# An attention and two feed-forward layers on one core: TensorE tile work in other groups, one PSUM pair shared in another way

## The chip, the cores and the metric

One core of one Trainium2 chip runs the whole program. The metric is the device time of one execution in microseconds; the kernel before took 1379.79 us, the median of three runs (1379.1 to 1381.74).

## The reference

```python
a   = softmax(phi, axis=2)                       # over 576 tokens, per memory slot
k_m = einsum('bhsm,bhsd->bhmd', a, k)            # 32 memory rows per head
v_m = einsum('bhsm,bhsd->bhmd', a, v)
attn = softmax(q @ k_m.T / 8, axis=-1)           # 576 x 32 per head
x = (attn @ v_m).transpose(0, 2, 1, 3).reshape(4608, 512)
h = x @ w_in;  x = (h * sigmoid(h)) @ w_out      # 512 -> 2048 -> 512
h = x @ w_in2; g = where(h > 0, h, exp(min(h, 0)) - 1)
out = g @ w_out2
```

There are 8 batches of 8 heads, 576 tokens, head width 64 and 32 memory slots. The weights come in as float64.

## The kernel before

**Stages.** A stretch written out by hand (FIRST) does batch 0's attention and first layer and brings in the first layer's weights. A planned stretch, about 97 to 703 us of the trace, then does the rest of batch 0, the attention and the first feed-forward layer of batches 1 to 7, and converts and splits the second layer's weights. A last stretch does the second feed-forward layer, nine blocks of 512 tokens.

**What sets the order.** `Plan` holds tasks with an engine, a cost, a rank and what they depend on, and `run` simulates the engines and issues every instruction in the order that comes out of it; on the chip each engine runs its instructions in that order. In the planned stretch the large products of TensorE get due times in order (`by_due`), and every other task must be ready 35 us (`AHEAD`) before the product that needs it. A `ring` stands for a buffer: a new user waits for the release by the user some places before it, and for the task that made the last one.

**Large products.** TensorE multiplies in float16 as three terms (`mm3`). `plan_in1` makes h = x·w_in for one batch as 16 products of 12 matmuls of 288 columns (tile `ph<-aT,u`); `plan_out1` multiplies by w_out with seven products in place of eight (`ph<-T,w1s`). Both use two PSUM slots `m0` and `m1` of two banks each.

**The attention of one batch, all between those products.**
- `mem_T` turns exp(phi) by transposes (`eT`; the last 64 tokens are `etail`), `mem_es` copies them out. `mem_kv` multiplies by k and v (`kvp`): ten chunks a batch, each four matmuls on four column tiles of 32, in one task with its own load (`kv`, three buffers). The last chunk of each half of the heads has 64 tokens, so 64 rows.
- `mem_pad`, `mem_kvT`, `mem_vT` scale and turn the result (`kvTp`, `kT`, `vT`).
- `scores` (`sc`) multiplies q by kT on two column tiles of 64: for each 64-token piece c, all four pairs of heads p, so four matmuls in a row on one tile. `att_*` make the softmax, `att_T` turns it back (`aTp`), `att_split` writes `aT`. Tokens come in three parts j of 256, 256 and 64; the part of 64 uses half of the partitions.
- `u_mm` (`up`) folds v_m into w_in: for each quarter f of the 2048 columns and each half g of the heads, eight matmuls of 512 columns on four column tiles of 32, one task each. `u_split` makes float16 hi and lo on ScalarE and VectorE (tile `u`). One `u` serves one batch; the next batch's overwrites it after the last product that reads it.

**PSUM.** Eight banks: four for `m0`, `m1`; two for tag `a` (`sc`, `aTp`), one for `u` (`up`), one for `c` (`eT`, `kvp`, `kvTp`). In FIRST and in the last stretch `a_tile` deals the same four in turn:

```python
if turn[1]:
    tag = "aauc"[k]
return ps_a.tile(shape, F32, tag=tag, name=name, bufs=2 if tag == "a" else 1)
```

Of the kernel before, what the change touches and what calls it, by code (L numbers as in the profile page):

```python
# [18 lines left out]
P = 128  # L19
B, H, S, D, M = 8, 8, 576, 64, 32  # L20
DM, DFF = 512, 2048
NG = 2
# [22 lines left out]
W2FROM, W2TO, AHEAD = 0.2, 0.95, 35  # L45
# [46 lines left out]
def attn_moe_moe(ctx: ExitStack, tc: tile.TileContext, qT, phiT, kvm, kvt, w1i, w1o, w2i, w2o, out):  # L92
# [37 lines left out]
    def a_tile(shape, name, tag="a"):  # L130

        k = turn[0] % 4
        turn[0] += turn[1]
        if turn[1]:
            tag = "aauc"[k]
        return ps_a.tile(shape, F32, tag=tag, name=name, bufs=2 if tag == "a" else 1)
# [65 lines left out]
    class Plan:  # L202
# [3 lines left out]
        def __init__(self, ahead=None, busy={}):  # L206
            self.tasks = []
            self.rings = {}
            self.gates = {}
            self.ahead = ahead  # L210
            self.busy = busy
            self.due = None
            self.main = []
            self.dues = {}
# [8 lines left out]
        def product(self, cost, rank, fn, deps=()):  # L223
            self.main.append(len(self.tasks))
            return self.add("PE", cost, rank, fn, deps)
# [39 lines left out]
        def run(self):  # L265
# [16 lines left out]
            order = []  # L282
            while len(order) < n:
# [18 lines left out]
                _, cost, _, fn, _, hold = self.tasks[i]  # L302
                end = start + cost
# [328 lines left out]

    def load_phi(b):
# [4 lines left out]
    def load_kv(b, g, c):  # L638

        t = two.tile([P, 4 * 2 * D], F32, tag="kv", name=f"kv{b}", bufs=NKV)  # L640
        if c < NC - 1:
            nc.sync.dma_start(out=t, in_=kvm[b, g, :, c])
        else:
            nc.sync.dma_start(out=t[:TAIL], in_=kvt[b, g])
        st[b]["kv", g, c] = t

    def load_kv_whole(b, tags):
        for g in range(NG):
# [4 lines left out]
            load_kv(b, g, NC - 1)  # L653
# [16 lines left out]
    def mem_T(b, g):  # L670

        z = st[b]
        if g < NG:
            ps = z["eT", g] = a_tile([P, NC - 1, P], "eT", "c")
            for c in range(NC - 1):
                nc.tensor.transpose(ps[:, c], z["phi"][:, g, c * P:(c + 1) * P], ident)  # L676
        else:
            ps = z["eT", g] = a_tile([P, NG, P], "etail", "c")
            for h in range(NG):
                nc.tensor.transpose(ps[:TAIL, h], z["phi"][:, h, (NC - 1) * P:], ident)  # L680

    def mem_es(b, g):
        z = st[b]
        if "es" not in z:
            z["es"] = big.tile([P, NG, NC, P], F32, tag="es", name=f"es{b}")
        ps = z.pop(("eT", g))
        if g < NG:
            copy("K0" if b else "T0", z["es"][:, g, :NC - 1], ps)
        else:
            copy("K0" if b else "T0", z["es"][:TAIL, :, NC - 1], ps[:TAIL])  # L690

    def mem_kv(b, g, c):
# [3 lines left out]
        r = P if c < NC - 1 else TAIL  # L696
        t = z.pop(("kv", g, c))
        for h in range(4):
            nc.tensor.matmul(  # L699
                z["kvp"][32 * h:32 * h + 32, g],  # L700
                z["es"][:r, g, c, 32 * h:32 * h + 32],
                t[:r, h * P:(h + 1) * P],
                start=(c == 0),
                stop=(c == NC - 1),
                tile_position=(0, 32 * h),
            )
# [76 lines left out]
    def tokens(j):  # L783

        return (P, 2) if j < 2 else (TAIL, 1)

    def scores(b, j):
        z = st[b]
        r, n = tokens(j)
        ps = z["sc", j] = a_tile([P, 2, H, M], "sc")  # L790
        for c in range(2 * n if j < 2 else 1):
            t0 = 256 * j + 64 * c
            o = 64 * (c % 2)
            for p in range(NP):
                nc.tensor.matmul(  # L795
                    ps[o:o + 64, c // 2, 2 * p:2 * p + 2],
# [7 lines left out]
    def att_max(b, j):  # L804
        z = st[b]
        r, n = tokens(j)
        sc = z["sc", j][:r, :n].rearrange("p n h m -> p (n h) m")
        z["smx", j] = small("smx", 16)
        nc.vector.tensor_reduce(out=z["smx", j][:r, :n * H], in_=sc, axis=AX.X, op=ALU.max)

    def att_sub(b, j):
        z = st[b]
        r, n = tokens(j)
        k = n * H
        sc = z.pop(("sc", j))[:r, :n].rearrange("p n h m -> p (n h) m")
        a = z["att", j] = two.tile(
            [P, 16, M], F32, tag="att" if b else "stage", name="att", bufs=2 if b else 4)
        tt(a[:r, :k], sc, z.pop(("smx", j))[:r, :k].unsqueeze(2).to_broadcast([r, k, M]), ALU.subtract)

    def att_exp(b, j):  # L820
        r, n = tokens(j)
        a = st[b]["att", j][:r, :n * H]
        nc.scalar.activation(out=a, in_=a, func=AF.Exp, scale=float(1.0 / np.sqrt(D)))

    def att_sum(b, j):
        r, n = tokens(j)
        k = n * H
        aa = st[b]["att", j][:r, :k]
        s1, s2 = small("ss1", 16), small("ss2", 16)
        st[b]["ss3", j] = small("ss3", 16)  # L830
        nc.vector.tensor_reduce(out=s1[:r, :k], in_=aa, axis=AX.X, op=ALU.add)
        nc.vector.tensor_scalar_add(s2[:r, :k], s1[:r, :k], 1e-9)
        nc.vector.reciprocal(st[b]["ss3", j][:r, :k], s2[:r, :k])

    def att_mul(b, j):
        r, n = tokens(j)
        k = n * H
        aa = st[b]["att", j][:r, :k]
        tt(aa, aa, st[b].pop(("ss3", j))[:r, :k].unsqueeze(2).to_broadcast([r, k, M]), ALU.mult)

    def att_T(b, j):
        z = st[b]
        r, n = tokens(j)
        a = z.pop(("att", j)).rearrange("p (n g h) m -> p n g (h m)", n=2, g=NG)
        ps = z["aTp", j] = a_tile([P, NG, 256], "aTp")
        for g in range(NG):
            for c in range(n):
                nc.tensor.transpose(ps[:, g, P * c:P * c + r], a[:r, c, g], ident[:r, :r])  # L848

    def att_split(b, j, lo):  # L850
        z = st[b]
        r, n = tokens(j)
# [3 lines left out]
        t = slice(256 * j, 256 * j + n * r)  # L856
        ps = z["aTp", j][:, :, :n * r]
# [23 lines left out]
    def u_mm(b, f, g):  # L881
# [3 lines left out]
        ps = z["up", f, g] = a_tile([P, FW], "up", "u")  # L885
# [26 lines left out]

    def plan_mem(pl, n, r, ex, ready):
# [10 lines left out]
        for g in range(NG + 1):  # L924
            t = on("PE", 0.5 if g < NG else 0.3, lambda g=g: mem_T(n, g), ex + pl.ring(*C))
            free = pl.take("c", t)
            phi_free.append(t)
            es.append(on("ACT", act(512 if g < NG else 256, False), lambda g=g: mem_es(n, g),
# [6 lines left out]
        for g in range(NG):  # L935
            for c in range(NC):
                load, free = [], []
                if n > 1:
                    load = [pl.load(256 if c < NC - 1 else 128, r - 300, lambda g=g, c=c: load_kv(n, g, c), pl.ring("kv", NKV), KVLATE if c < NC - 1 else 3.0)]
                    free = pl.take("kv", load[0])  # L940
                elif c == NC - 1:
                    free = pl.rings["kv"][1 + g][1]
                t = on("PE", 0.3, lambda g=g, c=c: mem_kv(n, g, c), load + es + (last or pl.ring(*C)))
                if not last:
                    kv_free = pl.take("c", t)
                last = [t]
                free.append(t)
            kv += last
# [25 lines left out]
    def plan_u(pl, n, r, mem, ready):  # L974
# [4 lines left out]
        for f in (0, 2, 1, 3) if n == 1 else range(NF):  # L979
            for g in range(NG):  # L980
                t = pl.add("PE", 0.55, r, lambda f=f, g=g: u_mm(n, f, g), [mem["vl"], ready["w1i", f]] + pl.ring("u", 1) + (
                    pl.ring(f"u{g}", 1) if f == 0 else [u[0, g]]))
                mem["vT_free"].append(t)
                free = pl.take("u", t)
# [7 lines left out]
    def plan_attn(pl, n, r, mem, after):  # L992


        A = "a", 2
# [10 lines left out]
        for j in range(3):  # L1006
            rows, w = tokens(j)
            k = 256 * w
            sc = on("PE", 1.8 if j < 2 else 0.5, lambda j=j: scores(n, j), [mem["kT"]] + qs + pl.ring(*A))
# [12 lines left out]
            t = on("PE", 0.6 if j < 2 else 0.3, lambda j=j: att_T(n, j), [t] + pl.ring(*A))  # L1022
# [39 lines left out]
    mslot = [0]  # L1062

    def ps_half(k):
        ps = ps_m.tile([P, 2, 512], F32, tag=f"m{k}", name="ph")
# [51 lines left out]
    def plan_in1(pl, b, r, A, u, u_free, first, h_free):  # L1117
# [4 lines left out]
        silus = []  # L1122
        at = mslot[0]

        def mm(m):
            w[m], ps = ps_half((at + m) % 2)
# [9 lines left out]
        for m in range(KF):  # L1136
            t = pl.product(1.475, r + m, lambda m=m: mm(m), A["aT"] + [u[m // 4, g] for g in range(NG)] + pl.ring(f"m{(at + m) % 2}", 1))
            for free in u_free + [A["aT_free"]]:
                free.append(t)
            free = pl.take(f"m{(at + m) % 2}", t)  # L1140
            silus.append(pl.add("ACT", act(S) - 0.02, r + m - 2000, lambda m=m: silu(m), [t, A["scales"]] + (silus[-1:] or first) + h_free(m)))
            free.append(silus[-1])
# [68 lines left out]
    def plan_out1(pl, b, r, silus, made, stored, scales, y_tile, y_ring, squares_rank=0):  # L1211
# [10 lines left out]
        SLOT = mslot[0], 1 - mslot[0]  # L1222
        mslot[0] = SLOT[1]
# [419 lines left out]
    def first_steps():  # L1643
# [29 lines left out]
        f["K0"] = lambda: ([mem_kv(0, g, c) for g in range(NG) for c in range(NC)], [mem_pad(0, g) for g in range(NG)])  # L1673
# [9 lines left out]
    def plan_first():  # L1683
# [79 lines left out]
        for k in range(NT):  # L1763
            pl.take("T", None).extend([ready["kv", 1][k]] if k < 2 else reads[3] + [done[KD - 1, 3]])
# [40 lines left out]
    with tc.manual_schedule():  # L1805
# [7 lines left out]
        turn[1] = 1  # L1813
        early.close()
# [78 lines left out]
```

## Time and profile before

| | us | share |
|---|---|---|
| median of three runs | 1379.79 | |
| the profiled execution | 1379.99 | |
| its span in the profile | 1378.2 | 1 |
| PE (TensorE) busy | 1351.3 | 98% |
| DVE (VectorE) busy | 1107.6 | 80% |
| ACT (ScalarE) busy | 952.3 | 69% |

The time of an execution holds 1.8 us around the span. A matmul's row shows its whole passage through the array, so rows of consecutive matmuls overlap; how long a block holds TensorE is read from its start to the start of the next block. A float32 matmul shows as two instructions.

### The profile page before, as it was taken

How to read it: one execution, taken by the hardware profiler on the slowest of the kernel's cores; microseconds unless marked ns; L12 is line 12 of the kernel's file. 1: busy time of each engine (PE TensorE's matmuls, PEld its weight loads, DVE VectorE, ACT ScalarE, POOL GpSimd, SP SyncE). 2: the span in 40 equal slices, each digit the busy share in tenths (PEclk: the TensorE clock that was granted, in tenths of full speed). 3: DMA queues.
4: the chain of work that ended last, by engine and by line, in shares of the span. 5: the costliest groups of instructions: out<-in, count | busy, mean ns of one | idle time of the engine just before them, and what ended most of it. 6: DMA issues, size and time to landing. Idle time of an engine off the chain costs nothing.

```text
span 1378.2 us, 28737 instructions
## 1 busy us (share of the span) xinstructions
PE 1351.3 (98%) x12105; PEld 1095.5 (79%) x12105; DVE 1107.6 (80%) x1730; ACT 952.3 (69%) x1366; POOL 84.6 (6%) x147
## 2 busy tenths in 40 slices
PE   7998999999999999999999999999999999999998
PEld 4676677776767767676787888888888888888887
DVE  6687788696988989697869797888879797879784
ACT  4757674967868686785658675758676676767672
POOL 0033100001010000011000000000000000000000
PEclk8999999999999999999999999999999999999999
DMA  9475857368576647645394242333333241514230
GB/s 371 175 253 169 291 213 267 124 236 280 188 246 236 237 161 265 255 151 209 122 372 150 78 142 76 124 100 100 109 108 116 69 154 43 171 53 134 87 99 31
DMA packets 65729, 233.07 MB, mean 169 GB/s; under 512 B 9024, under 2 KB 15168, under 8 KB 60992
## 3 DMA queue, kind: packets, MB, share of 16 engines
q1 hardware_dynamic: 53120, 187.19, 39.9%
q0 software_dynamic: 12480, 44.05, 8.4%
q8 instruction: 94, 1.54, 0.5%
q14 instruction: 35, 0.29, 0.1%
HBM read 186.12 MB, written 40.89 MB: 165 GB/s over the span
## 4 chain that ended last, share of the span: by engine, by line
PE 74%; DMA 3%; issue 3%; ACT 1%; DVE 1%; POOL 0%; ACTq 0%; SPq 0%; POOLq 0%
PE ph L1048 24%; PE o L1048 23%; PE h2A L1048 13%; PE h2D L1048 10%; DMA wi<-w2is 1%; PE sc L795 1%; DMA kv<-in_kvm 1%; PE up L889 1%; DMA w2is<-hl_q 1%; PE kvp L699 1%; PE aTp L848 0%; ACT h L1133 0%; DVE hl_q L189 0%; POOL w2is L468 0%; PE eT L676 0%
## 5 line engine op out<-in xcount | busy, mean ns | idle before, releaser
L1048 PE MATMUL o<-t,wq 128*128 128x256 f16 x3024 | 358.2, 273 | 0.1
L1048 PEld LDWEIGHTS <-wi 128*128 128x128 f16 x3024 | 295.6, 98 | 40.6 <-DMA wi<-w2is 4.4
L1048 PEld LDWEIGHTS <-wq 128*128 128x128 f16 x3024 | 295.8, 98 | 34.6 <-issue 0.3
L1048 PE MATMUL ph<-T,w1s 128*128 128x288 f16 x2352 | 301.7, 286 | 0.0
L1048 PEld LDWEIGHTS <-w1s 128*128 128x128 f16 x2352 | 225.9, 98 | 64.5 <-issue 8.4
L1048 PE MATMUL h2A<-xh,wi 128*128 128x256 f16 x1728 | 228.0, 273 | 4.5 <-DMA wi<-w2is 3.5
L1485 ACT ACTIVATE h<-h2A,inv 128x256 f32<-128x256 f32 x288 | 133.7, 468 | 136.2 <-PE h2A L1048 133.1
L1048 PE MATMUL ph<-aT,u 128*128 128x288 f16 x1344 | 174.5, 286 | 1.0 <-ACT h L1133 0.9
L189 DVE SCALAR_TENSOR_TENSOR t<-h,s_g,t 128x768 f16<-128x768 f32 (+1 forms) x144 | 164.0, 1146 | 13.6 <-ACT t L184 13.2
L1048 PE MATMUL h2D<-xh,wi 128*128 128x256 f16 x1296 | 172.8, 273 | 0.0
L1489 DVE SCALAR_TENSOR_TENSOR h<-h2D,inv,h 128x256 f32<-128x256 f32 x216 | 103.7, 481 | 77.2 <-PE h2D L1048 55.1
L1048 PEld LDWEIGHTS <-u 128*128 128x128 f16 x1344 | 127.5, 98 | 47.0 <-issue 16.1
L184 ACT ACTIVATE t<-h,s_g 128x768 f16<-128x768 f32 (+1 forms) x144 | 146.3, 1033 | 22.6 <-DVE h L148 11.5
L189 DVE SCALAR_TENSOR_TENSOR T<-h,c,T 128x1152 f16<-128x1152 f32 x98 | 136.8, 1412 | 10.6 <-ACT T L184 10.5
L148 DVE TENSOR_TENSOR h<-h 128x256 f32<-128x256 f32 (+1 forms) x302 | 129.4, 463 | 2.7
L184 ACT ACTIVATE T<-h,c 128x1152 f16<-128x1152 f32 x98 | 119.4, 1252 | 15.6 <-DVE h L148 10.0
L1133 ACT ACTIVATE h<-ph,inv 128x576 f32<-128x576 f32 x112 | 82.4, 737 | 22.7 <-PE ph L1048 22.2
L1527 DVE SCALAR_TENSOR_TENSOR h<-e,h 128x1024 f32<-128x1024 f32 x72 | 87.7, 1218 | 7.3 <-ACT e L1523 7.3
L1520 ACT ACTIVATE e<-h 128x1024 f32<-128x1024 f32 x72 | 75.5, 1049 | 9.1 <-DVE h L1489 8.1
L1523 ACT ACTIVATE e<-e 128x1024 f32<-128x1024 f32 x72 | 75.6, 1050 | 0.7
L1096 PE MATMUL ph<-h,w1o 128*128 128x288 f32 x256 | 66.8, 418 | 0.5 <-DVE w1o L345 0.5
L148 DVE TENSOR_TENSOR h<-h,h 128x1152 f32<-128x1152 f32 x42 | 56.6, 1354 | 10.7 <-ACT h L1133 10.4
(185 smaller groups left out, 1298.5 us busy)
## 6 DMA issues: line engine op xcount, KB each, us to landing
w1s<-w1os SPq DMA_DIRECT2D x98, 512.0 KB, 4.4
wi<-w2is SPq DMA_DIRECT2D x56, 896.0 KB, 4.7
kv<-in_kvm SPq DMA_DIRECT2D x48, 256.0 KB, 6.1
q<-in_qT SPq DMA_DIRECT2D x32, 288.0 KB, 7.7
raw<-in_w1i SPq DMA_DIRECT2D x8, 1024.0 KB, 13.5
raw<-in_w1o SPq DMA_DIRECT2D x8, 1024.0 KB, 4.9
raw<-in_w2i SPq DMA_DIRECT2D x8, 1024.0 KB, 6.4
raw<-in_w2o SPq DMA_DIRECT2D x8, 1024.0 KB, 7.1
```

What stands on the lines that cost most here:

```text
L148: nc.vector.tensor_tensor(out=out, in0=a, in1=b, op=op)
L184: nc.scalar.activation(out=hi, in_=x, func=AF.Copy, scale=s)
L189: nc.vector.scalar_tensor_tensor(out=lo, in0=x, scalar=s, in1=hi, op0=ALU.mult, op1=ALU.subtract)
L699: nc.tensor.matmul(z["kvp"][32 * h:32 * h + 32, g], z["es"][:r, g, c, 32 * h:32 * h + 32], t[:r, h * P:(h + 1) * P], start=(c == 0), stop= ...
L1048: nc.tensor.matmul(o, w, x[:, c], start=first, stop=last, **how)
L1096: nc.tensor.matmul(z[d][1][t], wB[d][:, k], h[k // KQ][:, t, k % KQ], start=(k == 0), stop=(k == KF - 1))
L1133: nc.scalar.activation(out=h[m // KQ][:, :, m % KQ], in_=w.pop(m), func=AF.Silu, scale=z["inv1"][:, m // 4:m // 4 + 1])
L1485: nc.scalar.activation(out=w["x"][:, s], in_=w["A"], func=AF.Copy, scale=inv)
L1489: return pl.add("DVE", COST["add"], base, lambda: nc.vector.scalar_tensor_tensor(out=w["x"][:, s], in0=w["D"], scalar=inv, in1=w["x"][:, s ...
L1520: nc.scalar.activation(out=w["e"], in_=w["x"][:, B21:], func=AF.Relu, scale=-1.0)
L1523: nc.scalar.activation(out=w["e"], in_=w["e"], func=AF.Exp, scale=-1.0)
L1527: nc.vector.scalar_tensor_tensor(out=x, in0=w["e"], scalar=-1.0, in1=x, op0=ALU.add, op1=ALU.max)
```

## The change

It has these parts; the core of the diff follows.
- PSUM: `a` has one bank; tag `u` is a tile of two banks. `u_mm` fills both banks (both halves of the heads) in one task, and `plan_in1` uses the same pair as a third slot `m2` for its products. FIRST and the last stretch deal the two banks of one such tile (`both`) in turn with `a` and `c`.
- The 16 products of `plan_in1` and the quarters of u go in the order of quarters 0, 2, 1, 3 for every batch.
- `scores` loops over p outside and c inside, so consecutive matmuls alternate between the two column tiles.
- The last 64 tokens: two halves of the heads lie on the two halves of the partitions (`etail`, the scores, `aTp`, `kvt`; `phi` of the second half is rolled by 64 tokens on the host). `etail` is one transpose and two copies, `aTp` of the tail is one transpose, the tail's k and v are one load of 128 rows.
- `mem_kv` runs in tasks of three chunks (all nine for batch 1); nine loads instead of ten.
- `Plan` marks column-tile tasks (`tiles`); after one, it takes another one if one is ready, and a change between kinds costs it `TURN`.
- Costs and the due times of the second layer's weights (`W2FROM`, `W2TO`) are other numbers.

```diff
-W2FROM, W2TO, AHEAD = 0.2, 0.95, 35
+UORDER = 0, 2, 1, 3
+MORDER = [4 * f + k for f in UORDER for k in range(4)]
+KVCOST = 0.0, 0.09
+TURN, DEFER, MANY = 0.095, 0.0, 1
+W2FROM, W2TO, AHEAD = 0.25, 0.98, 35
...
+    def pair_tile(name):
+        return ps_a.tile([P, 2, 512], F32, tag="u", name=name, bufs=1)
...
-                    i = min((i for i in r if at[i] <= start), key=lambda i: (self.tasks[i][2], i))
+                    can = [i for i in r if at[i] <= start]
+                    if eng == "PE" and self.tiled:
+                        part = [i for i in can if i in self.tiled]
+                        if tiled:
+                            can = part or can
+                        elif len(part) < MANY and all(start < at[i] + DEFER for i in part):
+                            can = [i for i in can if i not in self.tiled] or can
+                    i = min(can, key=lambda i: (self.tasks[i][2], i))
...
+                if eng == "PE" and (i in self.tiled) != tiled:
+                    tiled = not tiled
+                    cost, hold = cost + TURN, hold + TURN
...
-        for c in range(2 * n if j < 2 else 1):
-            t0 = 256 * j + 64 * c
-            o = 64 * (c % 2)
-            for p in range(NP):
+        for p in range(NP):
+            for c in range(4 if j < 2 else 1):
+                t0 = 256 * j + 64 * c
+                o = 64 * (c % 2 if j < 2 else p // 2)
...
+    def GROUPS(n):
+        return [CHUNKS] if n == 1 else [CHUNKS[i:i + NKV] for i in range(0, len(CHUNKS), NKV)]
...
-            for g in range(NG):
-                t = pl.add("PE", 0.55, r, lambda f=f, g=g: u_mm(n, f, g), [mem["vl"], ready["w1i", f]] + pl.ring("u", 1) + (
-                    pl.ring(f"u{g}", 1) if f == 0 else [u[0, g]]))
+            t = pl.tiles(0.9, r, lambda f=f: [u_mm(n, f, g) for g in range(NG)], [mem["vl"], ready["w1i", f]] + pl.ring("m2", 1) + (
+                pl.ring("u0", 1) + pl.ring("u1", 1) if f == 0 else [u[0, 0], u[0, 1]]))
...
-        A = "a", 2
+        A = "a", 1
...
-        ps = ps_m.tile([P, 2, 512], F32, tag=f"m{k}", name="ph")
+        ps = ps_m.tile([P, 2, 512], F32, tag=f"m{k}", name="ph") if k < 2 else pair_tile("ph")
...
+        slot = {m: ((2, 0, 1) if b == 1 else (1, 2, 0))[n % 3] for n, m in enumerate(MORDER)}
```

## Rows read from the trace of the kernel before

**Rows 1.** Stages: window, PE, PEld, DVE, ACT, POOL busy (instructions), PEclk, DMA, GB/s

```profile
97.00:703.00 606.00, 598.13 (x5496) 442.45 (x5488) 502.36 (x704) 429.71 (x621) 56.47 (x91) 0.99 0.63 220
703.00:1378.20 675.20, 665.83 (x6081) 594.30 (x6078) 539.01 (x906) 463.89 (x653) 19.14 (x35) 1.00 0.33 110
```

**Rows 2.** What PE waited for from 90 to 705 us: total, times, longest

```profile
PE kvTp L764 <- ACT pad L192: 4.7, 1, 4.7
PE kvp L699 <- DMA kv<-in_kvm: 2.1, 2, 1.6
PE ph L1048 <- ACT h L1133: 0.9, 2, 0.7
```

**Rows 3.** PE in order of time, 400 to 480 us: start, length, operation, instructions

```profile
401.96 0.42 PE L699 MATMUL kvp<-kv,es 128*32 128x128 f32 x8
402.32 1.65 PE L1048 MATMUL ph<-aT,u 128*128 128x288 f16 x12
403.89 0.61 PE L889 MATMUL up<-w1i_hl,vT 128*32 128x512 f16 x8
404.44 3.11 PE L1048 MATMUL ph<-aT,u 128*128 128x288 f16 x24
407.48 0.61 PE L889 MATMUL up<-w1i_hl,vT 128*32 128x512 f16 x8
...
467.35 0.68 PE L795 MATMUL sc<-kT,q 128*64 128x64 f32 x8
467.96 0.61 PE L889 MATMUL up<-w1i_hl,vT 128*32 128x512 f16 x8
...
476.65 0.65 PE L699 MATMUL kvp<-kv,es 128*32 128x128 f32 x16
477.11 0.61 PE L889 MATMUL up<-w1i_hl,vT 128*32 128x512 f16 x8
477.54 0.40 PE L699 MATMUL kvp<-kv,es 128*32 128x128 f32 x8
```

**Rows 4.** PE in order of time: blocks at the first and last change of tiling

```profile
97.76 0.42 PE L699 MATMUL kvp<-kv,es 64*32 64x128 f32 x8
...
656.11 0.61 PE L889 MATMUL up<-w1i_hl,vT 128*32 128x512 f16 x8
```

**Rows 5.** The chain that ended last, in order of time: start, length, one block

```profile
445.39 1.47 PE sc L795 x32
```

**Rows 6.** PE groups from 97 to 703 us: shapes, count, busy us, mean ns, idle before

```profile
L795 PE MATMUL sc<-kT,q 128*64 128x64 f32 x504 | 26.3, 228 | 0.0
L676 PE MATMUL eT<-ident,phi 128*128 128x128 f32 x48 | 7.6, 282 | 0.0
L848 PE MATMUL aTp<-ident,att 64*128 64x64 f32 x14 | 2.3, 247 | 0.0
L680 PE MATMUL etail<-ident,phi 128*64 128x128 f32 x12 | 2.3, 275 | 0.0
```

**Rows 7.** PE in order of time, first stage: scores and first product of batch 0

```profile
18.28 4.09 PE L795 MATMUL sc<-kT,q 128*64 128x64 f32 x66 [0.27 <-DMA q<-in_qT]
...
29.68 4.21 PE L1055 MATMUL ph<-aT,u 128*128 128x288 f32 x8
```

**Rows 8.** DVE in order of time, 440 to 520 us: vT ready, first u split

```profile
465.91 0.48 DVE L189 SCALAR_TENSOR_TENSOR vT<-kvTp,s_v,vT 128x256 f16<-128x256 f32 x1
...
471.20 0.68 DVE L189 SCALAR_TENSOR_TENSOR u<-up,u 128x512 f16<-128x512 f32 x1
```

**Rows 9.** Busy time by engine while one batch's second product and the next's first run

```profile
428.00:479.00 51.00, 51.00 (x496) 39.47 (x495) 47.39 (x68) 34.70 (x53) 2.04 (x2) 1.00 0.74 261
479.00:507.00 28.00, 28.00 (x269) 19.01 (x267) 21.71 (x31) 24.27 (x35) 2.86 (x5) 1.00 0.55 190
```

**Rows 10.** The kv tile from 97 to 703 us: its loads, issue to landing

```profile
DMA to landing us min/median/max: 2.5/6.2/12.7
```

**Rows 11.** Tile hl_q from 97 to 703 us: last stores of the second layer's weights

```profile
L464 POOL DMA_DIRECT2D w2os<-hl_q x14: 531/540/626, 493.4 to 651.6; - x14
```

More of the change, by code (lines that the diff above doesn't have):

```diff
@@ L212, in __init__ @@
             self.due = None
+            self.tiled = set()
             self.main = []
@@ L224, in product, with tiles @@
             self.main.append(len(self.tasks))
+            return self.add("PE", cost, rank, fn, deps)
+        def tiles(self, cost, rank, fn, deps=()):
+            self.tiled.add(len(self.tasks))
             return self.add("PE", cost, rank, fn, deps)
@@ L282, in run @@
             order = []
+            tiled = False
             while len(order) < n:
@@ L638, in load_kv @@
     def load_kv(b, g, c):
[L640 to L645, printed above, removed]
+        t = st[b]["kv", g, c] = two.tile([P, 4 * 2 * D], F32, tag="kv", name=f"kv{b}", bufs=NKV)
+        nc.sync.dma_start(out=t, in_=kvm[b, g, :, c] if c < NC - 1 else kvt[b])
     def load_kv_whole(b, tags):
@@ L675, in mem_T @@
             for c in range(NC - 1):
-                nc.tensor.transpose(ps[:, c], z["phi"][:, g, c * P:(c + 1) * P], ident)
+                nc.tensor.transpose(ps[:, c], z["phi"][:, g, TAIL * g + c * P:TAIL * g + (c + 1) * P], ident)
         else:
-            ps = z["eT", g] = a_tile([P, NG, P], "etail", "c")
-            for h in range(NG):
-                nc.tensor.transpose(ps[:TAIL, h], z["phi"][:, h, (NC - 1) * P:], ident)
+            ps = z["eT", g] = a_tile([P, P], "etail", "c")
+            nc.tensor.transpose(ps, z["phi"].rearrange("p g s -> p (g s)")[:, S - TAIL:S + TAIL], ident)
     def mem_es(b, g):
@@ L695, in mem_kv @@
             z["kvp"] = a_tile([P, NG, P], "kvp", "c")
-        r = P if c < NC - 1 else TAIL
         t = z.pop(("kv", g, c))
[L698 to L706, printed above, removed]
+        last = c == NC - 1
+        for g in range(NG) if last else (g,):
+            for h in range(4):
+                m = slice(32 * h, 32 * h + 32)
+                nc.tensor.matmul(
+                    z["kvp"][m, g],
+                    es_tail[:, g, m] if last else z["es"][:, (NC - 1) * g + c, m],
+                    t[:, h * P:(h + 1) * P],
+                    start=(g == 0 and c == 0 or g == 1 and last),
+                    stop=(g == 0 and last or g == 1 and c == NC - 2),
+                    tile_position=(0, 32 * h),
+                )
     def mem_sums(b):
@@ L841, in att_T @@
+        aa = st[b]["att", j][:, :k]
+        tt(aa, aa, st[b].pop(("ss3", j))[:, :k].unsqueeze(2).to_broadcast([P, k, M]), ALU.mult)
     def att_T(b, j):
         z = st[b]
-        r, n = tokens(j)
-        a = z.pop(("att", j)).rearrange("p (n g h) m -> p n g (h m)", n=2, g=NG)
-        ps = z["aTp", j] = a_tile([P, NG, 256], "aTp")
-        for g in range(NG):
-            for c in range(n):
-                nc.tensor.transpose(ps[:, g, P * c:P * c + r], a[:r, c, g], ident[:r, :r])
+        a = z.pop(("att", j))
@@ new lines, in att_T @@
+        if j < 2:
+            a = a.rearrange("p (n g h) m -> p n g (h m)", n=2, g=NG)
+            ps = z["aTp", j] = a_tile([P, NG, 256], "aTp")
+            for g in range(NG):
+                for c in range(2):
+                    nc.tensor.transpose(ps[:, g, P * c:P * c + P], a[:, c, g], ident)
+        else:
+            ps = z["aTp", j] = a_tile([P, NG, TAIL], "aTp")
+            nc.tensor.transpose(ps.rearrange("p g t -> p (g t)"), a[:, :H // 2].rearrange("p h m -> p (h m)"), ident)
@@ L934, in plan_mem @@
         kv = []
-        for g in range(NG):
-            for c in range(NC):
-                load, free = [], []
+        for cs in GROUPS(n):
+            loads, frees = [], []
+            for g, c in cs:
                 if n > 1:
-                    load = [pl.load(256 if c < NC - 1 else 128, r - 300, lambda g=g, c=c: load_kv(n, g, c), pl.ring("kv", NKV), KVLATE if c < NC - 1 else 3.0)]
-                    free = pl.take("kv", load[0])
+                    loads.append(pl.load(256, r - 300, lambda g=g, c=c: load_kv(n, g, c), pl.ring("kv", NKV), KVLATE))
+                    frees.append(pl.take("kv", loads[-1]))
                 elif c == NC - 1:
[L942 to L946, printed above, removed]
+                    frees.append(pl.rings["kv"][2][1])
+            t = pl.tiles(KVCOST[0] + KVCOST[1] * len(cs), r, lambda cs=cs: [mem_kv(n, g, c) for g, c in cs], loads + es + (last or pl.ring(*C)))
+            if not last:
+                kv_free = pl.take("c", t)
+            last = [t]
+            for free in frees:
                 free.append(t)
-            kv += last
+        kv = last
         es_free += last
@@ L1006, in plan_attn @@
         for j in range(3):
-            rows, w = tokens(j)
-            k = 256 * w
-            sc = on("PE", 1.8 if j < 2 else 0.5, lambda j=j: scores(n, j), [mem["kT"]] + qs + pl.ring(*A))
+            k = M * groups(j)
+            sc = pl.tiles(0.95 if j < 2 else 0.25, r, lambda j=j: scores(n, j), [mem["kT"]] + qs + pl.ring(*A))
             free = pl.take("a", sc)
@@ L1134, in silu @@
                 out=h[m // KQ][:, :, m % KQ], in_=w.pop(m), func=AF.Silu, scale=z["inv1"][:, m // 4:m // 4 + 1])
-        for m in range(KF):
-            t = pl.product(1.475, r + m, lambda m=m: mm(m), A["aT"] + [u[m // 4, g] for g in range(NG)] + pl.ring(f"m{(at + m) % 2}", 1))
+        last = first
+        for n, m in enumerate(MORDER):
+            t = pl.product(1.475, r + n, lambda m=m: mm(m), A["aT"] + [u[m // 4, g] for g in range(NG)] + pl.ring(f"m{slot[m]}", 1))
             for free in u_free + [A["aT_free"]]:
                 free.append(t)
-            free = pl.take(f"m{(at + m) % 2}", t)
-            silus.append(pl.add("ACT", act(S) - 0.02, r + m - 2000, lambda m=m: silu(m), [t, A["scales"]] + (silus[-1:] or first) + h_free(m)))
-            free.append(silus[-1])
+            free = pl.take(f"m{slot[m]}", t)
+            last = [pl.add("ACT", act(S) - 0.02, r + n - 2000, lambda m=m: silu(m), [t, A["scales"]] + last + h_free(m))]
+            silus[m] = last[0]
+            free += last
         return silus
@@ L1763, in plan_first @@
         for k in range(NT):
-            pl.take("T", None).extend([ready["kv", 1][k]] if k < 2 else reads[3] + [done[KD - 1, 3]])
+            pl.take("T", None).extend([ready["kv", 1][-1]] if k < 2 else reads[3] + [done[KD - 1, 3]])
         silus = []
@@ L1813, in attn_moe_moe @@
         turn[1] = 1
+        both[:] = [pair_tile("both")]
         early.close()
@@ L1868, in w2_out @@
         return quads(w.view(np.int64).reshape(2, KQ, P, 2, 2, P).transpose(4, 3, 0, 2, 1, 5))
+    phiT = phi.transpose(0, 1, 3, 2).reshape(B, NG, P, S).transpose(0, 2, 1, 3)
     kv = np.concatenate([k, v], axis=-1)
```

105 lines of the change are left out of this document (56 added, 49 removed).

## The prediction

> **What bounds the kernel now.** I read the stages first, since shares over the whole span mix them. Between 97 and 703 us TensorE is busy for 598.1 of 606 us, VectorE for 502.4, ScalarE for 429.7; in the last stretch TensorE is busy for 665.8 of 675.2 [rows 1]. So TensorE is the bound nearly everywhere, and a change pays if it takes time out of TensorE's queue without opening holes. Then I read what TensorE waited for: 7.7 us in the planned stretch, 4.7 of it one wait for ScalarE's `pad` [rows 2]. Waits have little to give. The order of TensorE's blocks shows what has: matmuls on column tiles stand as short blocks between the large products, and the turn from one kind to the other costs time that no busy share shows.
>
> That price: 12 matmuls of `ph` followed by a tiled block take 1.57 us from start to start (402.32 to 403.89), 24 take 3.04 (404.44 to 407.48). So 12 take 1.47, and turning to a tiled block costs 0.10. Turning back: `up` takes 0.55 when `ph` follows (403.89 to 404.44) and 0.43 when `kvp` follows (477.11 to 477.54), so 0.12 [rows 3]. I take 0.11 a turn. Walking that view from 97 to 703 us, counting every change between the whole array, 128x32, 64x32, 128x64 (scores) and 64x128 (the tail's transposes), gives 238 turns, the first at 97.76, the last after the block at 656.11 [rows 4]: 26 us.
>
> **The change part by part.**
>
> *Grouping.* Per batch there were eight blocks of `up`, ten of `kvp`, three of `sc` and one 64-row transpose pair; some already adjoined. Afterwards there are four of `up`, three of `kvp` (one in batch 1) and three of `sc`; the tail's transposes run on the whole array and its k and v on 128 rows. Seven batches: 28 + 19 + 21 = 68 blocks, 136 turns if none adjoin, perhaps 110 if the preference for another tiled task joins two a batch. I take 125: 113 fewer at 0.11 is 12.4 us (bounds 11.2 and 14.1). The matmuls themselves stay: the tail's k and v still take eight, on twice the rows.
>
> *Scores.* A block of eight instructions on one column tile takes 0.61 (467.35 to 467.96) [rows 3], less 0.12 for the turn 0.49, or 0.061 each. The block of 32 takes 1.47 [rows 5], less the turn 1.35; 32 at 0.061 would be 1.95, so some overlap happens already where the piece, and with it the tile, changes. What alternating tiles give is seen at `kvp`: 16 instructions of 128 columns on four tiles in turn take 0.46 (476.65 to 477.11), 0.029 each [rows 3]. A whole-array transpose of 128 columns adds 0.125: four in `eT` make a row of 0.63 (7.6 over 12 blocks), two in `etail` one of 0.38 (2.3 over 6) [rows 6]. That is a factor of four for four tiles, so I take two for two: 32 at 0.031 is 0.98, saving 0.37 in each of 14 blocks (504 instructions are 14 of 32 and 7 of 8 [rows 6]), 5.2 us. The tail's four matmuls, two on each half, go from 0.49 to some 0.30: 1.3. Together 6.5. No row shows two tiles of 64 in strict turn, so the bounds are 0 and half of today's time, 9.5 + 1.7 = 11.2.
>
> The Trainium skill's "TensorEngine Tiling (Array Packing)", section Theoretical Speedup, gives up to 2x for 64 columns. Taken from today's 1.35 that would be 0.68 a block and 4.2 us more in all, near 1357; the row says that part of this overlap is already there, and I go by the row.
>
> *Tails.* One transpose fewer in `etail` is 0.125 in six batches; the pair in `aTp` (2.3 over 7, 0.33 a row) becomes one of about 0.26 [rows 6]: 0.75 + 0.5, 1.2 us (0 to 2.3). The softmax of the tail works on twice the partitions and half the elements; ScalarE copies the tail in two pieces. Neither engine bounds this stretch, so I count nothing; without that cover it would be a few tenths a batch.
>
> *Third slot for the first product.* The two waits for `h` by ScalarE, 0.9 us [rows 2], go: 0.9 (0 to 0.9). It is not a gain beyond that, as TensorE hardly waits there. In return `up` needs this pair, and all four u tasks of a batch must have run and been split before its second product (batch 1: its first). Behind a waiting u task on TensorE's queue stand the large products themselves.
>
> *One bank for `a`.* Scores of part j+1 now wait until part j's `aTp` has been split. In the chain to `aT` that is some 2 us twice a batch, at the side of about 40 us of `ph<-T,w1s`; free as long as the chain starts early enough.
>
> *k and v in threes.* All three buffers belong to one task, so the next three loads leave SP only after the whole group's matmuls; behind them on SP stand `w1s`, `phi` and `q`. A load lands 6.2 us after issue, 12.7 at worst [rows 10]. Three groups with 8 to 13 us between them fit into the 80 us of a batch. There is one load fewer a batch, the same bytes.
>
> *Order of quarters; later due times.* Half a of the sums after the first product can start after eight products instead of twelve, which spreads VectorE's work. The second layer's conversion ends about 0.03 of 570 us later: the last store goes from 651.6 to about 670 [rows 11], and the last stretch begins at 703 [rows 1]; nothing, with 30 us of cover.
>
> *First stage.* Scores of batch 0 run serially for 4.0 us after q's last part came, and the first product starts at 29.68 [rows 7]. Alternating, with q's parts used as they come, the first part is ready up to 1.5 us earlier, and the softmax tail is 0.5 shorter: up to 2.0. The tail's k and v now come before the second half's chunks, some 0.8 later, hidden by q's arrival. The 4.7 us wait for `pad` [rows 2] may take the gain back. I take 1.0 (0 to 2.0). The last stretch deals the same four banks in another pairing: nothing.
>
> *New waits.* The order is a simulation's, and today it misses by 3.0 us in `kvp` and `ph` [rows 2]. With one bank for `a`, a shared pair for u and loads in threes I charge 3.0 (bounds 0 and 18, one microsecond for each of 18 groups of loads).
>
> *Sum.* 12.4 + 6.5 + 1.2 + 0.9 + 1.0 - 3.0 = 19.0. From the profiled execution's 1379.99 (span 1378.2 and 1.8 around it), which lies 0.2 over the median of 1379.79, that gives 1361.
>
> **The rivals.**
>
> *A. u comes too late (slower).* A half of `up` started at 467.96 and its low part ended at 471.88 [rows 3, 8]: 3.9 us of turnaround. A pair needs one more pass of both engines, about 4.6; four in series through one slot 18.5 us before the second product. Today the first product of that batch starts at 479.0, and vT was ready at 466.4 [rows 8], 12.6 us ahead. If nothing upstream moves, TensorE stands still for 6 us a batch: 42 us, 1403. It eats the whole gain from 2.7 us a batch on, that is if vT comes less than 16 us ahead. For it: VectorE is at 47.4 of 51 us while `ph<-T,w1s` runs and at 21.7 of 28 during the first product [rows 9], and u's splits move from the second into the first. Against it: the due times pull u's inputs 35 us ahead, scores ran at 445 [rows 5], so the turned k and v were there 20 us before vT was made, and the weight conversions can trade places with u's splits.
>
> The Trainium skill, "Trainium Kernel Development and Optimization", section Best Practices, warns that tiling speeds up TensorE but not the emptying of PSUM. That is this rival's direction; the numbers above stand on rows.
>
> *B. Part of the gain comes back as small waits.* VectorE has 502 us of work [rows 1] in a stretch that shrinks to some 586, 86%. One to one and a half microseconds lost a batch, 7 to 10 in all, gives 1368 to 1371. For it: rows 9's crowding. Against: today's waits are small at nearly the same load.
>
> *C. The change doesn't do what it says at the scores.* If strict turns bring no more overlap than today's order, 6.5 us stay: 1367.5. Against: `kvp`'s factor of four.
>
> *D. Nothing measurable.* B and C together, or A at 2.7 us a batch: about 1380.
>
> **How the numbers follow.** Forecast 58% (own range 1355 to 1365), B 18%, C 7%, D 6%, A 11%. The forecast, B and C are faster, with a little of B's upper end lost to D: faster 0.84, same 0.05, slower 0.11, where 0.2% (2.8 us) is about what a measurement of this kernel tells from no change. The range starts at 1352: 14.1 for turns, 11 for scores, 2 for tails and 1 for the third slot with no new wait are 28. It ends at 1373, where the bulk of B lies inside; A, D and B's end are left out, under 2 in 10.
>
> **What would show it.** Right: turns from 97 to 703 us near 125; `sc` blocks near 1.0 us from start to start before the turn; `up` in blocks of 16 and `kvp` in blocks of 24; waits of TensorE in that stretch under 11 us; the last stretch as long as before. Wrong: TensorE waiting for `u` splits or vT at the start of each first product (A), for `kv` loads at a group's head, or for `sc` and `aTp` banks (B); `sc` blocks still at 1.35 (C); a last stretch longer by more than 1 us.

## The result, and the profile after

The kernel after takes 1368.63 us, the median of six runs (1365.06 to 1371.97), against 1379.44 for the kernel before in the same session (six runs, 1378.38 to 1382.93): a ratio of 0.9917, interval 0.9895 to 0.9939. It is faster by 10.8 us where 19 were forecast. The profiled execution took 1371.49 (span 1369.7), 2.9 over that median, so between the two profiled executions the gain is only 8.5; stages are compared between it and the profiled execution before, 1379.99 (span 1378.2).

The stages of the kernel after, by windows, columns as in [rows 1]:

```profile
97.00:678.00 581.00, 572.58 (x5388) 437.45 (x5387) 494.88 (x700) 424.54 (x620) 55.54 (x88) 0.99 0.65 227
678.00:1369.70 691.70, 672.13 (x6081) 594.87 (x6078) 540.00 (x907) 465.24 (x653) 19.23 (x35) 1.00 0.32 107
```

The boundary between the planned and the last stretch is the first matmul of the second layer (the first `h2A<-xh`). It moved from 702.74 to 677.78 us, so the work ahead of it lost 25 us. The last stretch, with the same 6081 matmuls, grew from 675.5 to 691.9 us and gave 16.4 back. TensorE stood idle for 19.6 us of it, against 9.4 in [rows 1].

TensorE's queue in the kernel after, in order of time, in the same part of the program as [rows 3] and [rows 5] (scores 16 to 21 us earlier, `up` and `kvp` some 23):

```profile
424.05 1.15 PE L833 MATMUL sc<-kT,q 128*64 128x64 f32 x32
425.13 10.46 PE L1092 MATMUL ph<-T,w1s 128*128 128x288 f16 x84
...
444.13 1.05 PE L930 MATMUL up<-w1i_hl,vT 128*32 128x512 f16 x16
445.11 0.66 PE L709 MATMUL eT<-ident,phi 128*128 128x128 f32 x4
...
451.37 0.46 PE L833 MATMUL sc<-kT,q 128*64 128x64 f32 x8
451.76 0.54 PE L1092 MATMUL ph<-T,w1s 128*128 128x288 f16 x3
...
452.71 1.05 PE L930 MATMUL up<-w1i_hl,vT 128*32 128x512 f16 x16
453.58 0.83 PE L737 MATMUL kvp<-kv,es 128*32 128x128 f32 x24
```

Read it from start to start. `sc` now takes 1.08 (424.05 to 425.13) where [rows 5] has 1.47. `up` stands in blocks of 16, `kvp` in blocks of 24. The first `up` takes 0.98 with a whole-array `eT` behind it, the second 0.87 with `kvp` behind it: the turn back is 0.11, beside 0.12 in [rows 3]. Counted from 97 to 690 us there are 126 turns; there were 238.

What TensorE waited for in the kernel after from 97 to 678 us, columns as in [rows 2]:

```profile
PE aTp L885 <- DVE att L165: 3.9, 1, 3.9
PE kvp L737 <- DMA kv<-in_kvm: 1.9, 2, 1.2
PE ph L1092 <- ACT h L1175: 1.0, 2, 0.8
PE ph L1092 <- DVE aT L206: 0.7, 1, 0.7
PE sc L833 <- DVE armaxc L178: 0.6, 1, 0.6
```

With a sixth wait of 0.3 that is 8.4 us, beside the 7.7 of [rows 2]: the long wait for `pad` has become one for `att`, and nothing waits for u. The same view from 678 us on:

```profile
PE both L1092 <- DVE h L1532: 8.7, 15, 1.2
PE h2A L1092 <- DMA wi<-w2is: 3.7, 2, 3.0
PE h2A L1092 <- ACT h L1528: 1.6, 3, 0.6
PE o L1092 <- DVE t L206: 0.4, 1, 0.4
```

and of the kernel before, from 703 us on:

```profile
PE h2A L1048 <- DMA wi<-w2is: 3.5, 3, 1.6
PE h2A L1048 <- ACT h L1485: 1.0, 2, 0.6
```

The first line of the kernel after is new: fifteen times a matmul that writes `both` waits for VectorE. One of these waits in order of time, TensorE first, then VectorE (the bracket is the idle time before the instruction and what ended it):

```profile
1019.84 0.82 PE L1092 MATMUL both<-xh,wi 128*128 128x256 f16 x6
...
1021.80 0.82 PE L1092 MATMUL both<-xh,wi 128*128 128x256 f16 x6
1022.46 0.82 PE L1092 MATMUL h2A<-xh,wi 128*128 128x256 f16 x6
1024.45 0.82 PE L1092 MATMUL both<-xh,wi 128*128 128x256 f16 x6 [1.17 <-DVE h L1532]
1025.10 0.82 PE L1092 MATMUL o<-t,wq 128*128 128x256 f16 x6
```

```profile
1022.73 0.48 DVE L1532 SCALAR_TENSOR_TENSOR h<-both,inv,h 128x256 f32<-128x256 f32 x1 [0.81 <-PE both L1092]
...
1023.92 0.47 DVE L1532 SCALAR_TENSOR_TENSOR h<-both,inv,h 128x256 f32<-128x256 f32 x1
```

TensorE starts at 1024.45, 0.06 us after VectorE's read of 1023.92 has ended. That read is of the half filled at 1021.80. The half that TensorE now writes was filled at 1019.84 and read from 1022.73 to 1023.21, so it was free 1.2 us earlier. That earlier read was itself held up: by its bracket VectorE stood idle for 0.81 until TensorE's block of 1021.80, into the other half, had ended. A block of six needs 0.65 from start to start; this one took 1.99 (1022.46 to 1024.45), so the wait shown as 1.17 cost 1.34: a wait costs some 0.16 more than its idle time, because the row of the matmul before it still shows as busy. The semaphores of the compiled program say the same: in the last stretch it makes TensorE wait 34 times, before it writes one half of `both`, for VectorE's read of the *other* half (18 one way, 16 the other); not each of them stops TensorE. The halves lie in different banks and hold unrelated results, yet the reads and writes of this one tile are ordered as a whole.

The Trainium skill's "PSUM — Partial Sum Buffer", section "PSUM bank collisions raise a hardware error", asks to guard PSUM by bank and quadrant, and reports two engines on different banks running clean. By that rule these waits guard nothing the chip needs. In line with it, e1_split below, where the two banks are separate tiles, has none of these waits and takes 15.6 us less.

### The profile page after: what moved, and what is told of

Read it like the earlier page. It is cut to its first block, busy times and chain, and to the rows that moved or that the text cites. A ratio compares the mean times of both kernels' runs of the same rounds, so it can differ in the third digit from the quotient of the medians.

```text
span 1369.7 us, 28731 instructions
## 1 busy us (share of the span) xinstructions
PE 1335.2 (97%) x12089; PEld 1093.8 (80%) x12089; DVE 1102.5 (80%) x1731; ACT 951.1 (69%) x1374; POOL 85.3 (6%) x147
## 4 chain that ended last, share of the span: by engine, by line
PE 86%; DMA 5%; DVE 4%; ACT 3%; issue 1%; SPq 0%; POOL 0%; ACTq 0%; DVEq 0%; POOLq 0%
PE ph L1092 30%; PE o L1092 17%; PE h2A L1092 13%; PE both L1092 12%; PE h2D L1092 4%; PE up L930 2%; PE ph L1099 2%; PE ph L1138 2%; DMA w1i_hl<-w1i_hl 1%; PE sc L833 1%; DVE h L1532 1%; PE kvp L737 1%; DMA kv<-in_kvm 1%; DMA wi<-w2is 1%; DMA q<-in_qT 1%
## 5 line engine op out<-in xcount | busy, mean ns | idle before, releaser
L1092 PE MATMUL o<-t,wq 128*128 128x256 f16 x2160 | 273.2, 273 | 0.5 <-DVE t L206 0.4
L1092 PE MATMUL ph<-aT,u 128*128 128x288 f16 x1344 | 167.3, 286 | 1.7 <-ACT h L1175 1.0
L1092 PEld LDWEIGHTS <-u 128*128 128x128 f16 x1344 | 130.9, 98 | 36.7 <-issue 3.9
L1092 PE MATMUL both<-t,wq 128*128 128x256 f16 x864 | 117.5, 272 | 1.5 <-DVE h L1532 1.2
L1532 DVE SCALAR_TENSOR_TENSOR h<-both,inv,h 128x256 f32<-128x256 f32 x120 | 56.8, 481 | 59.9 <-PE both L1092 52.0
L1092 PE MATMUL both<-xh,wi 128*128 128x256 f16 x720 | 96.2, 273 | 7.6 <-DVE h L1532 7.6
L1092 PE MATMUL h2D<-xh,wi 128*128 128x256 f16 x576 | 76.7, 273 | 0.0
```

What stands on the lines that cost most here:

```text
L1092: nc.tensor.matmul(o, w, x[:, c], start=first, stop=last, **how)
L1532: return pl.add("DVE", COST["add"], base, lambda: nc.vector.scalar_tensor_tensor(out=w["x"][:, s], in0=w["D"], scalar=inv, in1=w["x"][:, s ...
```

## The experiments

All times stand beside runs of the kernel before on the same chip: 25 (median 1379.58) for e1 to e4, 7 (median 1379.3) for e5 to e8; ratios are to these. The kernel after was not timed again beside them. Differences from it, and of e6 to e8 from e1_split, are between sessions, in which the kernel before stayed within 0.3 us. Each trace is of one execution.

For the longer last stretch my theory was the pair tile; the rivals were weights that are ready later, and an order that is worse by itself.

**e1_split.** The kernel after, with two separate one-bank tiles in FIRST and in the last stretch; the planned stretch keeps the pair.

```diff
+    pairs = ctx.enter_context(ExitStack())
+    ps_u = [pairs.enter_context(tc.tile_pool(name="ps_u", bufs=1, space=PSUM, side="right"))]
...
+            if k % 2 and not both:
+                return ps_u[0].tile(shape, F32, tag=f"b{k // 2}", name=name, bufs=1)
...
-        both[:] = [pair_tile("both")]
+        both.clear()
+        pairs.close()
+        ps_u[0] = ctx.enter_context(tc.tile_pool(name="ps_b", bufs=1, space=PSUM, side="right"))
```

> The changed kernel, but FIRST and the last stretch deal two separate one-bank tiles in place of the two halves of one two-bank tile; the planned stretch is as it was. Theory: the last stretch (first matmul of the second layer to the end) grew from 675.5 to 691.9 us because TensorE, writing one half, waits for VectorE's read of the other half. Then this kernel's last stretch is 675 to 679 us, TensorE waits on these tiles under 1 us in all (8.7 in the changed kernel), and the time is about 1355 (1352 to 1358). Rival 1: the stretch grew because the second layer's weights are ready later (a 3.0 us wait for wi with a slow clock behind it): then only the waits on the halves move, the stretch stays at 686 to 692, and the time at 1366 to 1371. Rival 2: the order of the last stretch, planned from another state, is worse by itself: the same, no gain.

Measured: 1353.05 us (1351.05 to 1355.27), ratio 0.9822, interval 0.9796 to 0.9847. The second layer begins at 678.44 and lasts 674.6 us, about as before the change (675.5). Waits of TensorE in the last stretch of e1_split:

```profile
PE h2A L1096 <- ACT h L1532: 1.5, 3, 0.6
PE h2A L1096 <- DMA wi<-w2is: 1.2, 2, 0.8
PE o L1096 <- DVE t L210: 0.3, 1, 0.3
```

The waits for the halves are gone and with them the loss. FIRST adds nothing to it: the second layer begins 0.7 later, not earlier. Both rivals fall: this kernel keeps the changed planned stretch, with its later weights and the state that it leaves to the last stretch, and still loses nothing there. This version beats both kernels.

**e5_before_pair.** The other way round: the kernel before, where only the second and fourth tile dealt in the last stretch become the halves of one tile.

```diff
+            if both and k % 2:
+                return both[0][:, k // 2].rearrange("p (a b) -> p a b", a=2)
+            if both:
+                tag = "uc"[k // 2]
...
+        both.append(ps_u[0].tile([P, 2, 512], F32, tag="pair", name="both"))
```

> The kernel before, with one part of the change alone: in the last stretch the second and fourth tile of each turn are the two halves of one two-bank tile (the two banks of tag a), the first and third the tiles of tags u and c. Theory: TensorE again waits for VectorE's reads of the other half; the last stretch goes from 675.5 to 690 to 693 us, with 7 to 10 us of waits on these tiles, the rest of the trace as it was: about 1395. Rival: the loss needs something else of the change (later weights, the plan's other start), and this kernel stays within 4 us of the kernel before.

Measured: 1391.67 us (1389.46 to 1393.75), ratio 1.0088, interval 1.0068 to 1.0107: 12.4 us slower with only the dealing of these four banks changed, a little less than the expected 15. Its waits of TensorE from 700 us on:

```profile
PE both L1055 <- DVE h L1496: 8.7, 15, 1.2
PE h2A L1055 <- ACT h L1492: 1.5, 3, 0.6
PE h2A L1055 <- DMA wi<-w2is: 0.9, 1, 0.9
PE o L1055 <- DVE t L196: 0.4, 1, 0.4
```

The same fifteen waits, to the tenth. The last stretch takes 687.6 us (700.1 to 1387.7), 12.1 more than before. The fifteen waits hold 11.1 of it: 8.7 idle and some 2.4 on top, 0.16 each. Another 2.1 don't show as idle time: 16 matmuls that write `both` start 0.07 to 0.20 us late, each 0.05 us after a read of `both` by VectorE has ended. So the pair itself costs some 13 us. Against it TensorE waited 2.6 less for `wi` than in the kernel before (0.9 beside 3.5); some 1.5 lie in other short waits.

The traces of e3_ungroup and e4_no_third, whose last stretch is that of the kernel after, show the same 8.7 us in fifteen waits, and last stretches of 688.4 and 687.8 us. In the six traces without the pair it takes 674.3 to 677.1.

**e2_before_sc.** The kernel before with the two loops of the scores exchanged, nothing else.

```diff
-        for c in range(2 * n if j < 2 else 1):
-            t0 = 256 * j + 64 * c
-            o = 64 * (c % 2)
-            for p in range(NP):
+        for p in range(NP):
+            for c in range(2 * n if j < 2 else 1):
+                t0 = 256 * j + 64 * c
+                o = 64 * (c % 2)
```

> The kernel before, with only the two loops of the scores exchanged (pairs of heads outside, token pieces inside). Theory: alternating column tiles shortens each block of 32 from 1.47 to 1.08 us from start to start, and all of it reaches the end: 14 blocks by 0.39 are 5.5 us, so 1374 (1372.5 to 1375.5); the tail block of 8 stays at 0.61. Rival: a shorter block only lets TensorE arrive earlier at waits in a plan that counts 1.8 us for it, and the time moves by under 2 us.

Measured: 1371.42 us (ten runs, 1367.39 to 1377.17), ratio 0.9946, interval 0.9925 to 0.9966: 8.2 us faster, more than the expected 5.5. Its queue in order of time:

```profile
438.46 1.15 PE L795 MATMUL sc<-kT,q 128*64 128x64 f32 x32
439.54 2.62 PE L1048 MATMUL ph<-T,w1s 128*128 128x288 f16 x20
```

1.08 from start to start. From the first product of batch 1 to the second layer this saves 4.8 us, twelve blocks at 0.39 being 4.7. The surplus lies ahead: batch 1's first product starts at 153.17 instead of 157.51, of which 2.4 is batch 0's first product (27.31 instead of 29.68). The other 2 lie between these two products, where the granted clock reads 0.97 here and 0.95 before; by that difference 126 us would be some 2.5 us shorter (an estimate). Whether this belongs to the loops or to the execution, one trace cannot say.

**e3_ungroup.** The kernel after with one chunk of k and v in a task.

```diff
-        return [CHUNKS] if n == 1 else [CHUNKS[i:i + NKV] for i in range(0, len(CHUNKS), NKV)]
+        return [CHUNKS] if n == 1 else [[c] for c in CHUNKS]
```

> The changed kernel, with k and v of batches 2 to 7 in tasks of one chunk again (nine tasks a batch instead of three). Theory: 36 more tiled blocks, less those that the preference joins (some 6 to 12), so 48 to 60 more turns of 0.11 us: 5 to 7 us longer than the changed kernel in the planned stretch, about 1374. Rival: the loads in threes cost as much as the turns save (TensorE waits for a whole group's loads, 1.9 us in the changed kernel), and this kernel is within 2 us of the changed one.

Measured: 1378.68 us (ten runs), ratio 1.0006, interval 0.9989 to 1.0023: 10 us above the kernel after, where 5 to 7 were expected. There are 171 turns, 45 more, 5.0 us at 0.11. About as much is one kind of wait of TensorE from 97 to 688 us:

```profile
PE kvp L737 <- DMA kv<-in_kvm: 6.8, 2, 4.5
```

4.9 more than in the kernel after. So the rival falls: threes save turns and, in this pair of traces, did not wait longer for their loads. That single chunks wait more is not shown: the kernel before, with single chunks, has 2.1 in this row, and e1_split, with threes, has 3.6.

**e4_no_third.** The kernel after with the first product on two slots.

```diff
-        slot = {m: ((2, 0, 1) if b == 1 else (1, 2, 0))[n % 3] for n, m in enumerate(MORDER)}
+        slot = {m: (mslot[0] + n) % 2 for n, m in enumerate(MORDER)}
```

> The changed kernel, with the first product on two slots again; the pair of banks serves u alone. Theory: the third slot is worth only the waits for h that it took away, 0.9 us in the kernel before, so the time stays within 2 us of the changed kernel's 1368.6. Rival: sharing the pair makes u late, and this kernel is faster by 2 us or more. Rival 2: the third slot is what absorbs the blocks of u that no longer stand between the first products, and this kernel is slower by 3 us or more.

Measured: 1375.05 us (ten runs, 1372.28 to 1378.3), ratio 0.9978, interval 0.9963 to 0.9993; the second layer starts at 684.41, 6.6 later. My theory, that the slot is worth under 2 us, was wrong: the kernel is 6.4 us slower, as the second rival has it. Waits of TensorE from 97 to 684 us:

```profile
PE ph L1092 <- ACT h L1177: 4.0, 4, 2.9
PE aTp L885 <- DVE att L165: 4.0, 1, 4.0
PE aTp L888 <- DVE att L165: 1.7, 1, 1.7
```

The second row is as in the kernel after; the first has grown by 3.0, and the third is new. With two slots a late copy of `h` stops TensorE for up to 2.9 us; with three it has the length of one more product. All waits together are only 3.0 longer than in the kernel after (11.4 beside 8.4), but behind two of them matmuls run at half pace: the granted clock reads 0.54 from 323.8 to 327 us and 0.55 from 621 to 624. From the first product of batch 1 to the second layer this kernel takes 9.3 us more (537.0 beside 527.7): 3.7 of that is idle time, some 3 the half pace; the rest is not divided. It starts that stretch 2.7 earlier, so that 6.6 are left.

**e6_split_order.** e1_split with the quarters in the order 0, 1, 2, 3.

```diff
-UORDER = 0, 2, 1, 3
+UORDER = 0, 1, 2, 3
```

> The kernel with two one-bank tiles (1353.1), with the quarters of u and the first products in the order 0, 1, 2, 3. Theory: the order 0, 2, 1, 3 lets the sums for the second product start four products earlier, but TensorE hardly waits there, so the time stays within 2 us, 1351 to 1355. Rival: without it the second product's operands are late and TensorE waits at the start of each second product, 1 us or more in each of seven batches: 1360 or more.

Measured: 1360.3 us (1357.32 to 1360.69), ratio 0.9856, interval 0.9837 to 0.9875: 7 us slower than e1_split, where I expected under 2, and 7.5 and 8.4 slower than e7 and e8 of its own session, which have the order 0, 2, 1, 3. The second layer starts 5.3 later than in e1_split. Its waits of TensorE from 97 to 683.7 us:

```profile
PE aTp L889 <- DVE att L169: 6.3, 2, 3.5
PE ph L1096 <- ACT h L1179: 2.1, 3, 1.1
PE ph L1096 <- DVE aT L210: 2.0, 2, 1.0
```

In e1_split these three read 3.3, 1.0 and 0.7. The rival named the time, but its wait, for the second product's operands, is not among them: what comes late is `att` and `aT`, both made by VectorE. I take it that VectorE's work comes in a burst there; no run shows that apart.

**e7_split_w2 and e8_split_nopref.** e1_split with the old due times of the second layer's weights, and e1_split without the preference for another tiled task.

```diff
-W2FROM, W2TO, AHEAD = 0.25, 0.98, 35
+W2FROM, W2TO, AHEAD = 0.2, 0.95, 35
```

> The kernel with two one-bank tiles (1353.1), with the old due times of the second layer's weights (0.2 and 0.95). Theory: nothing waits for them before the last stretch, so 1351 to 1355. Rival: the earlier conversion crowds VectorE while u's splits moved into the second products, and TensorE waits for u or aT: 1358 or more.

```diff
-                        if tiled:
-                            can = part or can
-                        elif len(part) < MANY and all(start < at[i] + DEFER for i in part):
+                        if len(part) < MANY and all(start < at[i] + DEFER for i in part):
```

> The kernel with two one-bank tiles (1353.1), where the plan no longer takes another tiled task after a tiled one (the cost of a turn stays). Theory: in the changed kernel only two of 62 tiled segments hold two tasks of different kinds, so the preference hardly acts; turns stay within 6 of 126 and the time within 2 us, 1351 to 1355. Rival: the preference is what keeps turns low: 20 or more turns come back, 1356 or more.

Measured: 1352.76 us (1350.77 to 1354.21), ratio 0.9808, interval 0.9786 to 0.983, and 1351.86 us (1350.4 to 1354.31), ratio 0.9801, interval 0.9782 to 0.982. Neither can be told from e1_split. Without the preference there are 127 turns beside 126: the grouping sits in the tasks, which issue whole groups, and not in the choice between ready tasks.

## Why the prediction was right in kind and too high in the gain

**Turns: right.** 112 fewer were counted, 113 forecast; the price still reads 0.11. What the 112 are worth together was not tried alone; e3_ungroup gives back 45 of them.

**Scores: right.** A block lost 0.39, 0.37 forecast; a tail's block takes 0.39 (451.37 to 451.76), where it took 0.61 before: 0.22 less, 0.19 forecast. The group of the kernel after that answers to the first of [rows 6]:

```profile
L833 PE MATMUL sc<-kT,q 128*64 128x64 f32 x504 | 19.3, 226 | 0.8 <-DVE armaxc L178 0.6 <-ACT kT L209 0.3
```

The 504 instructions lost 7.0 us of busy time at an unchanged length of one: they overlap.

**Tails: nearly right.** From start to start, `etail` holds TensorE for 0.16 in the median, 0.22 before, six times; the tail's `aTp` for 0.16, 0.27 before, seven times: 1.1 us, 1.2 forecast. The 0.27 holds a turn, which the count of turns has too. They were not tried alone.

**First stage: under-sized.** Forecast 1.0 with 2.0 as the bound; the first product of batch 0 came 2.1 earlier. The queue of the kernel after, for [rows 7]:

```profile
14.20 1.28 PE L833 MATMUL both<-kT,q 128*64 128x64 f32 x24 [0.52 <-DVE kT L215]
16.78 0.70 PE L833 MATMUL both<-kT,q 128*64 128x64 f32 x8 [1.30 <-DMA q<-in_qT]
17.27 1.92 PE L833 MATMUL sc<-kT,q 128*64 128x64 f32 x32
...
27.55 2.21 PE L1099 MATMUL ph<-aT,u 128*128 128x288 f32 x8 [0.63 <-ACT aT L209]
```

Part of the scores now runs before q's last piece, as argued. e2_before_sc reaches 27.31 with the loops alone. The two traces differ in clock here: up to this product the granted clock reads 0.87 before and 0.81 after. Where it reads 1.00 (e3, e7, e8, all with the changed FIRST), the product starts at 25.6 to 25.8. So the change is worth more here than the 2.1, by how much is open.

**Third slot and order of quarters: mis-sized.** They stood at 0.9 and at no price. e4_no_third and e6_split_order show 6.6 and 5.3 us to the start of the second layer. Read from the waits before [rows 2], 0.9 was all there was to win; but those are the waits of a queue with more turns in it. Without the third slot the copies of `h` come late, without the order of quarters the softmax, and each late copy can cost more than its wait where half pace follows. That is the kind of wait that rival B has, and these two runs show the two parts holding part of it off.

**New waits: charged 3.0, came to 0.7** (8.4 beside 7.7). Rival A did not happen: the rows above hold no wait for u or vT. The time measured lies in the band of rival B, 1368 to 1371, but not by B's way: small waits in the planned stretch did not grow. The loads of k and v landed in 5.5 us in the median, 11.6 at worst, no later than in [rows 10]; the last store of the second layer's weights leaves at 639.6, earlier than the 651.6 of [rows 11], since the whole stretch has become shorter.

Without the 3.0, the prediction's terms add up to 22.0; 25 were measured ahead of the second layer: 17.6 of them from batch 1's first product on (545.2 to 527.7 us), 7.4 before it, where the granted clock of the two executions differs and not all need be the change's.

**The step that failed** is "The last stretch deals the same four banks in another pairing: nothing." The banks are the same; the tile is not. It cost 16.4 us by the profiled executions. Some 13 of them are the pair's, made up as in e5_before_pair. Another 1.4 are matmuls at half pace behind a load of `wi` that came late in this execution, in order of time:

```profile
726.16 2.74 PE L1092 MATMUL h2A<-xh,wi 128*128 128x256 f16 x12 [2.98 <-DMA wi<-w2is]
728.70 1.66 PE L1092 MATMUL both<-xh,wi 128*128 128x256 f16 x12
```

Twelve matmuls took 2.54 after that wait and 1.50 in the next block; undisturbed, six take 0.65. The waits for `wi` themselves add almost nothing: 3.7 us in all, 3.5 in the kernel before. The rest lies in other short waits. In e3_ungroup and e4_no_third, with the same last stretch, no wait for `wi` is above 1.8, and the stretch is 3.5 to 4.1 shorter than here. So late loads and the half pace behind them made up about that much of this one execution, as late loads made up part of the execution before. The prediction named a longer last stretch among the signs that would prove it wrong, and that is the sign that came. The profiled execution came out 10.5 over the forecast: the 16.4, less the 6 that the work ahead of the last stretch gained beyond the sum. The median, 2.9 lower, is 7.6 over. That it lies inside the stated range is in part luck: a cost priced at nothing met gains priced too low.

## What to carry to other kernels

When buffers are merged into one tile, list who writes and who reads each part: separate banks are only separate if the program orders them separately, and the pair tile did no harm where one task fills both halves (`up`: no wait for u in the rows), and cost some 13 us where the halves take turns. Waits read in the queue before a change can be too low for the denser queue after it: the third slot, priced at 0.9 from them, was worth 6.4. Matmuls on column tiles paid twice for their order here: once for each turn (0.11 us), once for standing in a row on one tile (0.39 us of 1.47 for a block of 32).

## What the runs showed of the chip

A turn of TensorE from the whole array to column tiles cost 0.10 us in the kernel before; a turn back cost 0.12 there and 0.11 in the kernel after. The Trainium skill's "TensorEngine Tiling (Array Packing)", section Key Properties, says that a change of tiling mode drains TensorE. The trace is in line with it and gives the price; the drain itself it does not show.

In the kernel after two waits, of 3.0 and 3.9 us, were followed by matmuls at half pace. Behind the first, the load of `wi` above, twelve matmuls took 0.21 each in place of 0.11, the lower of the two clock levels (1.2 and 2.4 GHz). The windows of the kernel after from there on (columns as in [rows 1]) show the granted clock at 0.69, both levels in one window, and then at 1.00:

```profile
726.00:731.00 5.00, 4.84 (x32) 3.79 (x33) 0.97 (x3) 0.87 (x3) 0.00 (x0) 0.69 0.12 17
731.00:736.00 5.00, 5.00 (x49) 4.48 (x47) 4.97 (x9) 4.60 (x7) 0.00 (x0) 1.00 0.44 166
```

Behind the second, for `att` at 119.4 us, the granted clock reads 0.64 up to 127. In e4_no_third it reads 0.54 and 0.55 behind waits of 2.9 and 1.7. Behind the wait of 1.17 at 1024.45 the six matmuls took their usual 0.65.
